# Attention and SoLU feed-forward on one core: loads of a whole batch in twelve transfers, block transposes one round sooner, weight conversion on VectorE

## The chip, the core and the metric

The kernel runs on one core of a Trainium2 chip. A core has a matrix engine (TensorE, "PE" in the profile, with its weight loads listed as "PEld"), a vector engine (VectorE, "DVE"), an engine for activation functions (ScalarE, "ACT"), a general engine (GpSimd, "POOL") and one that here only issues transfers (SyncE, "SP"). Each works through its own queue in program order and waits on semaphores for the others. Transfers between the chip's main memory and the on-chip memory, and within the on-chip memory, are issued from the queues of SP and ACT ("SPq" and "ACTq") and carried out by 16 DMA engines; an issue occupies the issuing engine's queue.

The metric is the device time of one execution in microseconds (us), as the median of several runs. A profile is of one execution.

## What is computed

Attention with a threshold, over 8 batches of 8 heads with 576 positions of 64 values, and then a feed-forward block over the 4608 rows of 512 values that come out of it. All of it is in 32-bit floating point; `w_in` and `w_out` arrive as 64-bit floating point.

```python
scores = scale * np.matmul(q, k.transpose(0, 1, 3, 2))
thresh = np.max(scores, axis=-1, keepdims=True) - tau
scores = np.where(scores >= thresh, scores, -1000000000.0)
scores = scores - np.max(scores, axis=-1, keepdims=True)
attn = np.exp(scores)
attn = attn / (np.sum(attn, axis=-1, keepdims=True) + 1e-09)
x = np.matmul(attn, v)          # then (B,H,S,D) -> (B*S, H*D)

h = x @ w_in
e = np.exp(h - np.max(h, axis=-1, keepdims=True))
sm = e / (np.sum(e, axis=-1, keepdims=True) + 1e-09)
solu = h * sm
ln = (solu - mean(solu)) / np.sqrt(var(solu) + 1e-06) * g_ln
out = ln @ w_out
```

## The kernel before

**Tiles and rounds.** Two heads form a pair, so a batch has four pairs. The 576 query positions are four tiles of 128 and a rest of 64; position 4p+t lies on partition p of tile t. A batch is worked in two halves. In half 0 each pair is a *unit* of two rounds (query tiles 0 and 1 of both heads), in half 1 a unit of three (tiles 2 and 3, then the two rests in one tile). That makes 20 rounds to a batch and 160 rounds in all, called slots, numbered from 0; batch b starts at slot 20 b. The whole order of work is written out by hand in one loop over rounds (from L541); nothing reorders it.

**One slot's way through the engines.** PE makes the scores of two tiles into two of three score banks (`scores`, L277). DVE takes the row maxima (`maxes`, L287), POOL adds tau (`nth`, L291), ACT shifts the scores out of the bank with a steep slope below the threshold (L304), which frees the bank, and exponentiates them with a row sum (L311). One round later POOL adds the small constant to the sum, DVE takes the reciprocal (L321), and POOL scales the probabilities (`normalise`, L323). Two rounds after the scores, DVE transposes 32 x 32 blocks of them into a tile T (`blocks`, L337). When a unit is complete, SP issues 16 transfers that put the blocks of T in place, into a tile wT (L345). Five rounds after the unit's last scores (`LAG_PV`, L485) PE multiplies wT with v (`attend`, L363), and ACT and DVE copy the result (L373 to L381).

**Loads and turns.** `load(i)` brings one pair: q and k in two transfers each, v in one, and a transfer each for the rests qe, ke and ve, eight in all (L108, L115, L119). For batch 0 the first two pairs go through SP's queue at the start; everything after goes through ACT's, at the top of a round, ahead of that round's `exps`, four rounds before the pair is turned. `prep(i, step)` turns a pair on PE in three steps (q, k, the rests; L223, L234) with copies to qT and kT on ACT (L229, L231) and of the rests to q_end and kT on DVE (L238, L242). The q and k tiles are double, the v tiles sevenfold.

**The feed-forward block** works on 36 tiles of 128 rows, each over four rounds: two halves of `ff_h` (PE, L399), `ff_max` (DVE, L406), `ff_exp` (ACT, L412), `ff_mul` (DVE, L418), `ff_stats` (DVE and POOL, L428 to L439), `ff_t`, which turns u on PE (L450) and copies it to uT on ACT or DVE (L453), two halves of `ff_o` (PE, L463), and `ff_out` (ACT, L470) with its store (L479).

**One round** issues, in this order: loads that are due, `scores` and `maxes` of this slot, one job of a list (attend before turning u before prep, by `x_next`), early jobs (`ff_max`), `exps` of this slot, `normalise` of the slot before, late jobs (`ff_exp`, `ff_mul`, `ff_stats`, `ff_out`), a quarter of the feed-forward matmuls, `blocks` of the slot two before, a second job of the list, and in the first rounds a weight piece.

**Weights.** 16 pieces of 128 x 512 are loaded as 64-bit words and converted by integer arithmetic: `weight_a` takes the exponent and the mantissa apart (L170 and L180 on DVE, L174 and L177 on POOL), `weight_b` puts the 32-bit number together (L194 to L200, DVE). One piece is converted per round, up to slot 14; `center` then subtracts the mean from w_out (L210, L212).

**Banks.** Jobs of the list (turned q and k, turned u, the attend result) share two banks, of which the feed-forward result holds one for two rounds. A bank is free when the copy that reads it has ended.

Of the kernel before, what the change touches and what calls it, by code (L numbers as in the profile page):

```python
# [16 lines left out]
P = 128  # L17
# [3 lines left out]
def kernel(  # L21
# [59 lines left out]

    pairs = {}
    units = {}
    xh = {}
# [15 lines left out]
    def load(i, queue=nc.scalar):  # L100
        b, hp = divmod(i, NP)
        d = {}
        for nm, src in (("q", q), ("k", k), ("v", v)):
            hs = src[b, 2 * hp : 2 * hp + 2]
            bufs = 7 if nm == "v" else 2
            if nm == "v":
                t = loads.tile([P, 2, 4, D], F32, tag=nm, bufs=bufs, name=nm)
                queue.dma_start(  # L108
                    out=t.rearrange("p h t d -> p h (t d)"),
                    in_=hs[:, 0:SM, :].rearrange("h (p t) d -> p h (t d)", t=4),  # L110
                )
            else:
                t = loads.tile([P, 4, 2, D], F32, tag=nm, bufs=bufs, name=nm)
                for h in range(2):
                    queue.dma_start(  # L115
                        out=t[:, :, h], in_=hs[h, 0:SM, :].rearrange("(p t) d -> p t d", t=4)
                    )
            e = loads.tile([ST, 2, D], F32, tag=nm + "e", bufs=bufs, name=nm + "e")
            queue.dma_start(out=e, in_=hs[:, SM:S, :].rearrange("h p d -> p h d"))  # L119
            d[nm], d[nm + "e"] = t, e  # L120
        pairs[i] = d
# [36 lines left out]
    def weight_load(x):  # L158
        raw = work.tile([P, 512], I64 if wide else F32, tag="u", name="raw")
        nc.scalar.dma_start(out=raw, in_=piece(x)[0])  # L160
        raws[x] = dict(raw=raw)

    def weight_a(x):
        if not wide:
            return
        d = raws[x]
        hi = d["raw"].bitcast(I32).rearrange("p (n two) -> p n two", two=2)[:, :, 1]
        d["em"] = em = work.tile([P, 2, 512], I32, tag="uT", name="em")
        e, m = em[:, 0], em[:, 1]
        nc.vector.tensor_scalar(  # L170
            out=e, in0=hi, scalar1=20, scalar2=0x7FF,
            op0=ALU.logical_shift_right, op1=ALU.bitwise_and,
        )
        nc.gpsimd.tensor_scalar(  # L174
            out=e, in0=e, scalar1=896.0, scalar2=0.0, op0=ALU.subtract, op1=ALU.max
        )
        nc.gpsimd.tensor_scalar(  # L177
            out=e, in0=e, scalar1=255.0, scalar2=8388608.0, op0=ALU.min, op1=ALU.mult
        )
        nc.vector.tensor_scalar(  # L180
            out=m, in0=hi, scalar1=0xFFFFF, scalar2=0x100000,
            op0=ALU.bitwise_and, op1=ALU.bitwise_or,
        )
# [32 lines left out]
    def prep(i, step):  # L216
        d = pairs[i]
        tag, tp = take_bank("tp_" + "qke"[step])
        banks_free.append(tag)
        if step < 2:  # L220
            nm = "qk"[step]
            for t in range(4):
                nc.tensor.transpose(  # L223
                    out=tp[:, P * t : P * t + P], in_=d[nm][:, t],
                    identity=ident,
                )
            d[nm + "T"] = heads.tile([P, SM if step == 0 else S], F32, tag=nm + "T", name=nm + "T")
            if step == 0:
                nc.scalar.activation(out=d["qT"], in_=tp, func=AF.Copy, scale=scl)  # L229
            else:  # L230
                nc.scalar.copy(out=d["kT"][:, 0:SM], in_=tp)  # L231
            return
        for x, nm in enumerate("qk"):
            nc.tensor.transpose(  # L234
                out=tp[:, ST * x : ST * x + ST], in_=d[nm + "e"], identity=ident[0:ST, 0:ST]
# [6 lines left out]
        nc.vector.tensor_copy(out=d["kT"][:, SM:S], in_=tp[:, ST : 2 * ST])  # L242

# [54 lines left out]
    def exps(s):  # L298
# [3 lines left out]
        for x, (ps, _) in enumerate(d["ps"]):  # L302
            w = work.tile([P, S], F32, tag="w", bufs=7, name="w")
# [46 lines left out]
    def attend(key):  # L350
        b, half, hp = key
        i = b * NP + hp
        d = pairs[i]
# [4 lines left out]
        for c in range(5):  # L358
            kk = slice(0, P if c < 4 else ST)
            for h in range(2):  # L360
                vv = d["v"][:, h, c] if c < 4 else d["ve"][:, h]
# [5 lines left out]
        if hp == 0:  # L367
            xh[b, half] = work.tile([P, NP, 256], F32, tag="xh", bufs=4, name="xh")
# [39 lines left out]
    def ff_exp(t):  # L408
        d = ffn[t]
        d["u"] = work.tile([P, DFF], F32, tag="u", name="u")  # L410
# [31 lines left out]
    def ff_t(t, f):  # L442
        d = ffn[t]
        if f == 0:
            d["uT"] = work.tile([P, NC, P], F32, tag="uT", name="uT")
# [42 lines left out]
    loads_due = []  # L488
    prepped = {}

    def prep_job(i, step):
        prep(i, step)
        prepped[i] = step

    for i in range(NPAIR):
        b, hp = divmod(i, NP)
        if b == 0:
            at = [max(0, 2 * hp - 3 + x) for x in range(3)]
            loads_due.append((0, i))
        else:  # L500
            s0 = PER_BATCH * (b - 1) + HALF0 + 3 * hp + 1
            at = [s0, s0 + 1, s0 + 2]
            loads_due.append((s0 - 4, i))
        if i > 0:
            for step in range(3):
                x_jobs.append([at[step], 2, (lambda i=i, step=step: prep_job(i, step))])
# [11 lines left out]
    with tc.manual_schedule():  # L518
        load(0, nc.sync)
        loads_due.pop(0)  # L520
# [3 lines left out]
        load(1, nc.sync)  # L524
        loads_due.pop(0)
        weight_a(0)
        for step in range(3):
            prep_job(0, step)
# [4 lines left out]
        done_w = 1  # L533

# [6 lines left out]
        while True:  # L541
            if rnd < NS:
                while (
                    loads_due
                    and loads_due[0][0] <= rnd
                    and prepped.get(loads_due[0][1] - 2) == 2
                ):
                    load(loads_due.pop(0)[1])
# [49 lines left out]
            if rnd - 2 >= 0 and rnd - 2 in live:  # L598
                blocks(rnd - 2)
# [44 lines left out]
```

## Time and profile before

| | |
|---|---|
| median of 3 runs | 1339.88 us (1337.8 to 1340.06) |
| the profiled execution | 1342.53 us |
| its span, first to last instruction | 1340.7 us |
| mean granted clock of PE | 0.888 of full |
| busy share of PE, DVE, ACT, POOL | 84%, 50%, 43%, 31% |
| moved by DMA | 132.05 MB, 98 GB/s on average |
| transfers wT from T | 1024, issued by SP |
| loads of q, k, v and their rests on ACT's queue | 240 |

A row of the timeline gives the start and the duration in us, the engine, the line, the operation, the tile written and the tiles read, and how many such instructions were merged; in brackets stands the time for which the engine was idle before it and what ended that. A row of the waits gives who waited for whom, the total in us, how often, and the longest. "issue" names a wait for which the profile shows no releaser. A busy PE may run below its full clock, so its share says how long it was occupied and not how much it did.

### The profile page before, as it was taken

How to read it: one execution, taken by the hardware profiler on the slowest of the kernel's cores; microseconds unless marked ns; L12 is line 12 of the kernel's file. 1: busy time of each engine (PE TensorE's matmuls, PEld its weight loads, DVE VectorE, ACT ScalarE, POOL GpSimd, SP SyncE). 2: the span in 40 equal slices, each digit the busy share in tenths (PEclk: the TensorE clock that was granted, in tenths of full speed). 3: DMA queues.
4: the chain of work that ended last, by engine and by line, in shares of the span. 5: the costliest groups of instructions: out<-in, count | busy, mean ns of one | idle time of the engine just before them, and what ended most of it. 6: DMA issues, size and time to landing. Idle time of an engine off the chain costs nothing.

```text
span 1340.7 us, 13897 instructions
## 1 busy us (share of the span) xinstructions
PE 1129.8 (84%) x4209; PEld 542.9 (40%) x4209; DVE 671.0 (50%) x1241; ACT 574.3 (43%) x1169; POOL 417.4 (31%) x833
## 2 busy tenths in 40 slices
PE   5566798888988889879888889889878889997878
PEld 3233343444434444434434434444434444443333
DVE  4665564535535556445544546454545546654312
ACT  2333244444535445444534445445444445543211
POOL 6667232322323223222222223232223223332100
PEclk8567898779889899879988999889998999998899
DMA  6556135334344443534363433544353433333210
GB/s 169 134 152 154 41 88 122 98 92 101 92 110 103 100 92 82 125 96 99 74 148 93 105 78 85 133 100 98 77 142 96 103 82 86 99 88 74 67 38 23
DMA packets 261738, 132.05 MB, mean 98 GB/s; under 512 B 99352, under 2 KB 255008, under 8 KB 261664
## 3 DMA queue, kind: packets, MB, share of 16 engines
q1 hardware_dynamic: 169632, 86.78, 28.0%
q10 hardware_dynamic: 92032, 44.39, 12.5%
q8 instruction: 34, 0.56, 0.2%
q14 instruction: 40, 0.33, 0.1%
HBM read 36.70 MB, written 9.44 MB: 34 GB/s over the span
## 4 chain that ended last, share of the span: by engine, by line
PE 51%; SPq 13%; ACT 9%; DVE 9%; DMA 8%; issue 5%; POOL 3%; ACTq 1%; DVEq 0%
PE pv L363 14%; PE h_ps L399 13%; SPq L345 12%; PE o_ps L463 11%; PE s_ps L277 9%; DMA wT<-T 5%; ACT w L304 3%; ACT w L311 3%; DVE T L337 3%; DVE u L418 2%; DVE nm L287 2%; PE tp_u L450 1%; ACT u L412 1%; POOL em L174 1%; DMA q<-in_q_dram 1%
## 5 line engine op out<-in xcount | busy, mean ns | idle before, releaser
L287 DVE TENSOR_REDUCE nm<-s_ps 128x1 f32<-128x576 f32 x288 | 204.4, 744 | 211.4 <-PE s_ps L277 211.2
L304 ACT ACTIVATE w<-s_ps,nth 128x576 f32<-128x576 f32 x288 | 199.3, 738 | 229.9 <-POOL nth L291 192.1
L277 PE MATMUL s_ps<-kT,qT 64*128 64x64 f32 (+1 forms) x1024 | 226.5, 485 | 81.2 <-ACT w L304 75.5
L463 PE MATMUL o_ps<-w,uT 128*128 128x512 f32 x576 | 274.5, 622 | 1.0 <-ACT uT L453 1.0
L323 POOL TENSOR_SCALAR w<-w,sm 128x576 f32<-128x576 f32 x288 | 214.0, 754 | 179.7 <-DVE sm L321 179.7
L363 PE MATMUL pv<-wT,v 128*64 128x384 f32 (+1 forms) x1024 | 198.5, 544 | 75.9 <-DMA wT<-T 44.7
L399 PE MATMUL h_ps<-w,xh 128*128 128x512 f32 x512 | 249.5, 633 | 0.0
L291 POOL TENSOR_SCALAR nth<-nm,tau_t 128x2 f32<-128x2 f32 (+1 forms) x160 | 47.9, 299 | 592.5 <-DVE nm L287 591.1
L311 ACT ACTIVATE w<-w,ntau 128x576 f32<-128x576 f32 x288 | 220.4, 772 | 1.0
L277 PEld LDWEIGHTS s_ps<-kT,qT 64*128 64x128 f32 x1024 | 126.2, 204 | 218.7 <-issue 96.1
L337 DVE STREAM_TRANSPOSE T<-w 128x576 f32<-128x576 f32 x288 | 207.0, 753 | 13.6 <-DMA wT<-T 8.0
L463 PEld LDWEIGHTS o_ps<-w,uT 128*128 128x128 f32 x576 | 108.7, 198 | 129.1 <-issue 125.4
L363 PEld LDWEIGHTS pv<-wT,v 128*64 128x64 f32 x1024 | 90.5, 170 | 148.4 <-issue 127.7
L399 PEld LDWEIGHTS h_ps<-w,xh 128*128 128x128 f32 x512 | 98.6, 203 | 116.5 <-issue 115.7
L378 ACT COPY xh<-pv 64x256 f32<-64x256 f32 x32 | 11.7, 365 | 187.1 <-PE pv L363 167.1
L418 DVE TENSOR_TENSOR u<-h_ps,u 128x1024 f32<-128x1024 f32 x36 | 44.1, 1224 | 91.0 <-ACT u L412 91.0
L373 ACT COPY xh<-pv 128x256 f32<-128x256 f32 x32 | 11.9, 372 | 157.6 <-PE pv L363 129.2
L380 DVE COPY xe<-pv 64x64 f32<-64x64 f32 x32 | 6.9, 215 | 140.5 <-ACT xh L379 140.4
L321 DVE RECIPROCAL sm<-sm 128x2 f32<-128x2 f32 (+1 forms) x160 | 26.1, 163 | 98.4 <-POOL sm L320 96.7
L450 PE MATMUL tp_u<-ident,u 128*128 128x128 f32 x288 | 48.5, 295 | 24.7 <-ACT uT L453 10.7
L311 ACT ACTIVATION_READ_ACCUMULATOR w<-w,ntau 128x1 f32 x288 | 56.5, 196 | 0.0
L450 PEld LDWEIGHTS tp_u<-ident,u 128*128 128x128 f32 x288 | 35.3, 150 | 48.8 <-issue 19.8
(62 smaller groups left out, 801.1 us busy)
## 6 DMA issues: line engine op xcount, KB each, us to landing
wT<-T SPq DMA_DIRECT2D x512, 80.0 KB, 2.2
wT<-T SPq DMA_DIRECT2D x256, 100.0 KB, 2.3
wT<-T SPq DMA_DIRECT2D x256, 64.0 KB, 2.1
out_dram<-ob ACTq DMA_DIRECT2D x32, 256.0 KB, 2.6
q<-in_q_dram ACTq DMA_DIRECT2D x60, 128.0 KB, 2.9
k<-in_k_dram ACTq DMA_DIRECT2D x60, 128.0 KB, 2.9
v<-in_v_dram ACTq DMA_DIRECT2D x30, 256.0 KB, 3.2
raw<-in_moe_w_in_dram ACTq DMA_DIRECT2D x8, 512.0 KB, 3.7
```

The lines of the kernel that those rows point to most:

```text
L277: nc.tensor.matmul(out=ps[:, ks], lhsT=lhsT, rhs=kT[hh, ks], start=True, stop=True)
L287: nc.vector.tensor_reduce(out=nm[:, x : x + 1], in_=ps[:, 0:S], axis=AX.X, op=ALU.max, negate=True)
L304: nc.scalar.activation(out=w, in_=ps[:, 0:S], func=AF.Prelu, bias=d["nth"][:, x : x + 1], scale=1.0, alpha=1.0e30,)
L311: nc.scalar.activation(out=w, in_=w, func=AF.Exp, bias=ntau, scale=1.0, accum_out=sm[:, x : x + 1])
L323: nc.gpsimd.tensor_scalar(out=w, in0=w, scalar1=d["sm"][:, x : x + 1], scalar2=1.0, op0=ALU.mult, op1=ALU.mult,)
L337: nc.vector.transpose(out=T[:, :, place, :], in_=w)
L345: nc.sync.dma_start(out=wT[32 * c : 32 * c + 32, 0:nj, a, :], in_=T[32 * a : 32 * a + 32, c : NB : 4].rearrange("p j t q -> p j (t q)"),)
L363: nc.tensor.matmul(out=y[hh, 0 : 4 * nq], lhsT=vv, rhs=wT[kk, c, :, 64 * h : 64 * h + nq], start=c == 0, stop=c == 4,)
L399: nc.tensor.matmul(out=h[:, f], lhsT=x[:, c], rhs=w1[:, c, f], start=c == 0, stop=c == NP - 1)
L418: nc.vector.tensor_tensor(out=d["u"], in0=d["h"], in1=d["u"], op=ALU.mult)
L450: nc.tensor.transpose(out=tp[:, P * c : P * c + P], in_=d["u"][:, x : x + P], identity=ident)
L463: nc.tensor.matmul(out=d["o"], lhsT=d["uT"][:, c], rhs=w2[:, c], start=c == 0, stop=c == NC - 1)
```

## The change

There are three parts and some tiles that make room for them.

1. **Loads.** `load(b)` brings a whole batch in twelve transfers: q and k in four each (one per tile t, all heads), and one each for v, qe, ke and ve. It is a generator that is advanced once per round, so that a round issues at most two of them, over seven rounds; it starts when all pairs of the batch before are turned. For batch 0, q and k come in one transfer per head, q on SP's queue and k on ACT's. The q and k tiles of a batch are single, those of v double.
2. **Order.** `blocks` takes the slot one before instead of two before, in the round in which that slot is normalised. `LAG_PV` is unchanged. The w tiles go from seven to five.
3. **Weight conversion.** The two operations on POOL go to DVE.

Raw weights use the tiles xh2 and xh3, the exponents and mantissas u and uT; u and uT are single where they were double.

```diff
-    def load(i, queue=nc.scalar):
-        b, hp = divmod(i, NP)
+    def load(b):
         d = {}
         for nm, src in (("q", q), ("k", k), ("v", v)):
-            hs = src[b, 2 * hp : 2 * hp + 2]
-            bufs = 7 if nm == "v" else 2
+            bufs = 2 if nm == "v" else 1
+            e = loads.tile([ST, H, D], F32, tag=nm + "e", bufs=bufs, name=nm + "e")
...
+        if b == 0:
+            for h in range(H):
+                for nm, src, queue in (("q", q, nc.sync), ("k", k, nc.scalar)):
+                    queue.dma_start(
+                        out=d[nm][:, :, h], in_=src[b, h, 0:SM, :].rearrange("(p t) d -> p t d", t=4)
+                    )
+                if h == 1:
...
+                    yield
+        else:
+            for nm, src in (("q", q), ("k", k)):
+                for t in range(4):
+                    nc.scalar.dma_start(
+                        out=d[nm][:, t],
+                        in_=src[b, :, 0:SM, :].rearrange("h (p t) d -> t p h d", t=4)[t],
+                    )
+                    if t % 2:
+                        yield
+                nc.scalar.dma_start(
+                    out=d[nm + "e"], in_=src[b, :, SM:S, :].rearrange("h p d -> p h d")
                 )
+                yield
+        nc.scalar.dma_start(
+            out=d["v"].rearrange("p h t d -> p h (t d)"),
+            in_=v[b, :, 0:SM, :].rearrange("h (p t) d -> p h (t d)", t=4),
+        )
+        nc.scalar.dma_start(out=d["ve"], in_=v[b, :, SM:S, :].rearrange("h p d -> p h d"))
+        yield
...
-        nc.gpsimd.tensor_scalar(
+        nc.vector.tensor_scalar(
             out=e, in0=e, scalar1=896.0, scalar2=0.0, op0=ALU.subtract, op1=ALU.max
         )
-        nc.gpsimd.tensor_scalar(
+        nc.vector.tensor_scalar(
             out=e, in0=e, scalar1=255.0, scalar2=8388608.0, op0=ALU.min, op1=ALU.mult
         )
...
-            w = work.tile([P, S], F32, tag="w", bufs=7, name="w")
+            w = work.tile([P, S], F32, tag="w", bufs=5, name="w")
...
-        d["u"] = work.tile([P, DFF], F32, tag="u", name="u")
+        d["u"] = work.tile([P, DFF], F32, tag="u", bufs=1, name="u")
...
-            d["uT"] = work.tile([P, NC, P], F32, tag="uT", name="uT")
+            d["uT"] = work.tile([P, NC, P], F32, tag="uT", bufs=1, name="uT")
...
-        load(0, nc.sync)
-        loads_due.pop(0)
+        first = load(0)
+        next(first)
         constants()
         weight_load(0)
         weight_load(1)
-        load(1, nc.sync)
-        loads_due.pop(0)
+        for _ in first:
+            pass
         weight_a(0)
...
-                while (
-                    loads_due
-                    and loads_due[0][0] <= rnd
-                    and prepped.get(loads_due[0][1] - 2) == 2
-                ):
-                    load(loads_due.pop(0)[1])
+                if loaded + 1 < B and rnd >= PER_BATCH * loaded and turned == NP * (loaded + 1):
+                    loaded += 1
+                    loading = load(loaded)
+                next(iter(loading), None)
                 scores(rnd)
                 maxes(rnd)
...
-            if rnd - 2 >= 0 and rnd - 2 in live:
-                blocks(rnd - 2)
+            if rnd >= 1 and rnd - 1 in live:
+                blocks(rnd - 1)
```

61 lines of the change are left out of this document (29 added, 32 removed).

## The prediction

> **What bounds the kernel now.** I read the page's first parts, then a table of stages, then who waits for whom, then the timeline at the waits.
>
> ```profile
> PE 1129.8 (84%) x4209; PEld 542.9 (40%) x4209; DVE 671.0 (50%) x1241; ACT 574.3 (43%) x1169; POOL 417.4 (31%) x833
> ...
> PE 51%; SPq 13%; ACT 9%; DVE 9%; DMA 8%; issue 5%; POOL 3%; ACTq 1%; DVEq 0%
> ```
>
> TensorE (PE) is the fullest engine, but only half of the chain that ended last is PE. The table of stages (columns: stretch, its length, busy time of PE, PEld, DVE, ACT, POOL, granted clock, DMA share, GB/s) shows two regimes, the weight stage, then one batch like another:
>
> ```profile
> 0.00:128.70 128.70, 77.53 (x252) 41.87 (x252) 77.32 (x150) 45.62 (x92) 84.63 (x90) 0.67 0.58 151
> 345.80:499.20 153.40, 132.10 (x505) 63.32 (x504) 75.80 (x141) 70.61 (x144) 42.88 (x96) 0.90 0.42 100
> 1109.40:1250.30 140.90, 127.55 (x496) 59.08 (x496) 74.80 (x135) 65.45 (x135) 42.43 (x97) 0.94 0.33 80
> ```
>
> In the first 128.7 us POOL is the fullest; later PE is, with about 21 us of waiting per batch (153.4 less 132.1) at a clock below 1. The waits of PE after 160 us:
>
> ```profile
> PE pv L363 <- DMA wT<-T: 42.7, 15, 4.8
> PE s_ps L277 <- ACT w L304: 40.2, 21, 6.0
> PE pv L363 <- issue: 30.9, 8, 5.4
> PE tp_u L450 <- ACT uT L453: 10.7, 3, 5.5
> ```
>
> So two things stop PE: probabilities that arrive late (wT), and an ACT that is late with the shift of the scores (L304), whose end frees the score banks.
>
> **Block transposes a round sooner.** One late wT, slot 53 of the 160 rounds (POOL, DVE, SP's queue, PE):
>
> ```profile
> 458.03 0.74 POOL L323 TENSOR_SCALAR w<-w,sm 128x576 f32<-128x576 f32 x1 [0.29 <-DVE sm L321]
> ...
> 471.17 0.77 DVE L337 STREAM_TRANSPOSE T<-w 128x576 f32<-128x576 f32 x1
> ...
> 472.00 10.59 SPq L345 DMA_DIRECT2D wT<-T  x16
> ...
> 484.70 4.38 PE L363 MATMUL pv<-wT,v 128*64 128x384 f32 x16 [3.06 <-DMA wT<-T]
> ```
>
> The input was scaled at 458.8, yet its transpose ran at 471.2, because it stood behind the next round's feed-forward work on DVE. Then SP needs 10.6 us to issue 16 transfers, and PE lost 3.06 us. A round sooner it could run at about 459.5, which moves the landing forward by some 11 us, more than the longest wait (4.8). SP can take it: it holds nothing but wT transfers after the start, and it idles long enough for T:
>
> ```profile
> SPq L345 <- DVE T L337: 503.2, 49, 31.2
> ```
>
> The wT buffer of two units before is freed by an attend that stands earlier in the same round, so I cost that at nothing; uncovered it would be one pv block, 3 to 4 us of SP. Gain: 42.7 us, and of the eight "issue" waits two that are also wT. The other six are 3.82 us each (22.9 of 30.9) and stay: PE there wants a bank that DVE's last copy frees:
>
> ```profile
> 438.80 0.23 DVE L242 COPY kT<-tp_e 128x64 f32<-128x64 f32 x1
> ...
> 439.13 2.73 PE L363 MATMUL pv<-wT,v 128*64 128x256 f32 x16 [3.82 <-issue]
> ...
> 442.84 5.73 PE L463 MATMUL o_ps<-w,uT 128*128 128x512 f32 x8
> ```
>
> So 42.7 + 8.0 = **50.7 us**, in 17 waits.
>
> **Loads.** Today a pair's eight transfers stand in a row on ACT's queue, ahead of that round's exps:
>
> ```profile
> 229.47 1.30 ACTq L115 DMA_DIRECT2D k<-in_k_dram  x2
> 231.96 0.63 ACTq L119 DMA_DIRECT2D ke<-in_k_dram  x1
> ...
> 233.95 1.37 ACT L304 ACTIVATE w<-s_ps,nth 128x576 f32<-128x576 f32 x2 [6.93 <-DMA k<-in_k_dram]
> ...
> 234.75 1.85 PE L277 MATMUL s_ps<-kT,qT 64*128 64x512 f32 x3 [3.82 <-ACT w L304]
> ...
> 542.41 0.90 PE L450 MATMUL tp_u<-ident,u 128*128 128x128 f32 x3 [5.53 <-ACT uT L453]
> ...
> 1001.08 1.85 PE L277 MATMUL s_ps<-kT,qT 64*128 64x512 f32 x2 [6.01 <-ACT w L304]
> ```
>
> Each issue is about 0.63 us of ACT's sequencer, with a pause (230.77 to 231.96) where an issue waited. Afterwards a batch has 12 issues in place of 32, at most two (1.3 us) in a round. The PE waits of this kind: four on L304, first 3.82 and last 6.01, 19.8 us together, and two on uT (10.0 of the 10.7 us). **29.8 us**, in 6 waits. The remaining issues: today's 36 output tiles are stored by single short issues, after which PE has the waits of the second row:
>
> ```profile
> 453.51 0.36 ACTq L479 DMA_DIRECT2D out_dram<-ob  x1
> ...
> PE tp_u L450 <- ACT ob L470: 3.0, 4, 1.0
> ...
> q<-in_q_dram ACTq DMA_DIRECT2D x60, 128.0 KB, 2.9
> ```
>
> That is 0.083 us of PE per 0.36 us of issue; 49 groups (seven rounds in each of seven batches) of up to 1.3 us cost by that row about 49 x 0.083 x 3.6 = **15 us** back (nothing, if ACT's idle time covers all; 64 us if every group reaches PE). The q and k tiles are now single, but the next load waits until all four pairs are transposed, which is some eight rounds ahead of its first reader; the last k transfer still has some three. A transfer is 256 KB rather than 128 KB: today's land in 2.9 us (third row), and three rounds of 7.7 us (153.4 / 20) hide even four times that.
>
> **Clock.** A wait costs PE more than itself. After the 3.82 us above, eight o_ps matmuls took 5.73 us; undisturbed:
>
> ```profile
> 430.31 3.60 PE L463 MATMUL o_ps<-w,uT 128*128 128x512 f32 x8
> ...
> 460.94 2.80 PE L363 MATMUL pv<-wT,v 128*64 128x384 f32 x16
> ```
>
> That is 2.1 us more, and after the 3.06 us wait sixteen pv took 4.38 in place of 2.80, 1.6 more. I take 1.85 us for 21 of the 23 waits removed (the two shortest, under 2 us, left out): **38.9 us**. The Trainium skill (page TensorE: Matmul & The Clock Gate, section HAM oscillation — how this bites in real kernels) lets the clock fall only behind idle gaps longer than about 3.4 us; by that rule ten waits count (the four longest on wT, up to the 4.8 and 5.4 in the rows above, and the six of the loads) and the term is 18.5 us, not 38.9. The row of 3.06 us speaks against so sharp a limit, so I keep 21.
>
> **DVE's new wait.** Now each transpose follows POOL's scaling in the same round. The weight stage shows the order:
>
> ```profile
> 44.46 0.17 DVE L321 RECIPROCAL sm<-sm 128x2 f32<-128x2 f32 x1 [2.46 <-POOL sm L320]
> 44.54 1.42 DVE L337 STREAM_TRANSPOSE T<-w 128x576 f32<-128x576 f32 x2
> 45.89 0.84 DVE L194 SCALAR_TENSOR_TENSOR w<-raw,em 128x512 f32<-128x512 uint32 x1
> ...
> 47.98 0.42 DVE L170 TENSOR_SCALAR em<-raw 128x512 int32<-128x512 int32 x1
> 48.31 0.42 DVE L180 TENSOR_SCALAR em<-raw 128x512 int32<-128x512 int32 x1
> 48.65 1.41 DVE L287 TENSOR_REDUCE nm<-s_ps 128x1 f32<-128x576 f32 x2
> 53.26 0.17 DVE L321 RECIPROCAL sm<-sm 128x2 f32<-128x2 f32 x1 [3.20 <-POOL sm L320]
> ...
> 44.73 1.47 POOL L323 TENSOR_SCALAR w<-w,sm 128x576 f32<-128x576 f32 x2 [0.30 <-DVE sm L321]
> 48.48 2.03 POOL L174 TENSOR_SCALAR em<-em 128x512 int32<-128x512 int32 x1 [2.29 <-DVE em L170]
> 50.60 1.93 POOL L177 TENSOR_SCALAR em<-em 128x512 int32<-128x512 int32 x1
> 52.63 0.30 POOL L291 TENSOR_SCALAR nth<-nm,tau_t 128x2 f32<-128x2 f32 x1
> ...
> DVE nm L287 <- PE s_ps L277: 211.2, 80, 9.8
> ```
>
> The columns are start, duration, engine, line; the fence has DVE's rows, then POOL's, then one row of DVE's waits. Transposes that end at 45.96 would end at 44.73 + 1.47 + 0.77 = 46.97 (POOL's two scalings, then the second transpose): 1.0 us later. Queued behind them on DVE are the copies of q_end, kT and uT, which free banks, and the next round's max, on which nth, L304 and PE's next scores hang. In 72 rounds (36 tiles, two each) feed-forward work on DVE fills the gap; 88 remain. In half of all rounds (80 of 160) DVE is 2.6 us ahead of PE and hides it. So 44 x 1.0 = **44 us** back; between nothing and 88.
>
> **Weight stage.** The round is 8.80 us (reciprocal at 44.46, the next at 53.26), because nth stands on POOL behind two conversions of 2 us. On DVE they are the same kind of operation on the same tile as L170 and L180, which follow each other every 0.34 us; I take that. The new round, from reciprocal to reciprocal: transposes end after 2.51, three conversions 2.09 (45.89 to 47.98), four more 4 x 0.34 = 1.36, max 1.41, then 0.1 + 0.63 (52.63 to 53.26) for nth and the sum, and every third round some 0.8 us of copies: 8.4 us. DVE takes POOL's place as the bound: 0.4 x 13 rounds = 5 us gained. At 0.77 us an operation, the spacing after L194, the round is 10.1, and 13 x 1.3 = 17 us are lost. At the start ACT issues eleven more transfers before its first copy (11 x 0.63 = 7 us), but the block of eight that round 0 has today (5 us) goes: -2, with 5 us either way. Batch 1 is then loaded in rounds 6 to 12, its k and ke right ahead of their transposes, where two landings of 2.9 us may show: -3, from -6 to 0. Together **0** (from -30 to +8).
>
> **Single buffers.** u and uT go from two buffers to one, w from seven to five. The exp that rewrites u stands two rounds behind the transposes that read it, PE's own order puts the last reader of uT ahead of the transposes of the next tile, and w is free a round sooner. I cost that at nothing; if a cover failed, a wait like the 5.53 us on uT above would return.
>
> **Sum.** 50.7 + 29.8 + 38.9 + 0 - 15 - 44 = 60.4 us. The profiled execution took 1342.53 us (its span is 1340.7); the median of three, 1339.88, is 2.65 us below it. 1342.53 - 60.4 - 2.65 = 1279.5, so **1279 us**.
>
> **Rivals.**
> - Only wT gains: the loads still hold ACT, as an issue beside a wT burst waits in turn (the pause at 230.77). 50.7 + 15 x 1.85 - 15 - 44 = 19 us: 1320. For it: SP's 10.6 us of issue nearly fill a unit of two rounds; against: never more than two in a row. 0.16.
> - DVE's slack hides its wait: no 44 us, 1235. For it: DVE is 50% busy; against: it also waits for ACT and POOL. 0.14.
> - Only long gaps slow the clock: ten of the 21 waits exceed 3.4 us, so 11 x 1.85 = 20 us less, 1299. 0.06. The rule of the Trainium skill's page named above gives this.
> - **Slower**: DVE's wait for the scaling becomes the bound. Where max comes late PE waits for L304, and from some 2.5 us of waiting the clock falls too: 1.0 + 1.85 = 2.85 us a round. All else gains 104 us, so it decides from 37 rounds; at 50 of the 88 it is 142 us, a loss of 38: 1378. For it: in the weight stage DVE is already the next bound; against: the 2.6 us lead. 0.15.
> - The same rival near its turning point: no change beyond 0.2%, which is about what a measurement of this kernel can tell apart. 0.05.
>
> **How the numbers follow.** Forecast 0.44, its own range 1245 to 1310. Faster 0.44 + 0.16 + 0.14 + 0.06 = 0.80, same 0.05, slower 0.15. The range of 1215 to 1350 starts where nothing is given back and the weight stage gains its 8 us (1279 - 59 - 8 = 1212), takes in the weight stage at its worst (1309) and the second case, and ends just inside the slower case; it leaves out most of that case and a little below, about 0.2.
>
> **What would show it.** PE's waits on wT nearly gone, and pv's landing margin near 10 us: the first step. No ACT wait on a load over 2 us: the second. Batches of about 144 us in place of 153 and a clock near 0.93: the third. DVE's T waiting for POOL L323 about 1 us a time: the fourth. Rounds of 8.4 us in the first 130 us: the fifth. It is wrong if PE's waits on L304 grow past 80 us, or if T's waits are several us long.

## The result and the profile after

| | before | changed |
|---|---|---|
| median of 4 runs, us | 1339.97 (1337.8 to 1341.46) | 1224.29 (1221.78 to 1225.07) |
| profiled execution, us | 1342.53 | 1225.07 |
| its span, us, and mean granted clock | 1340.7, 0.888 | 1223.2, 0.935 |

The ratio is 0.9135, with a 95% interval of 0.9116 to 0.9153: 115.7 us are gained where 60 were forecast. The time lies inside the range, near its lower end. Line numbers of the changed kernel are 24 to 29 above those of before (L304 becomes L333, L337 becomes L366).

The page's first parts of the changed kernel, busy times and chain:

```profile
PE 1090.5 (89%) x4209; PEld 525.1 (43%) x4209; DVE 690.2 (56%) x1273; ACT 574.8 (47%) x1169; POOL 350.8 (29%) x801
...
PE 53%; DVE 13%; DMA 9%; ACT 8%; SPq 6%; issue 5%; POOL 4%; ACTq 1%; DVEq 0%
```

PE's share of the span has gone from 84 to 89%, and SP's queue has lost more than half of its share of the chain (13 to 6%). The table of stages says more. I cut each run where PE starts the first scores of batch 1 (slot 20). Before that the weights are converted; behind it every batch does the same work. First the two rows of before, then those of the changed kernel (length, then busy times of PE, PEld, DVE, ACT and POOL):

```profile
0.00:192.30 192.30, 128.27 (x408) 65.34 (x408) 109.96 (x213) 67.82 (x137) 105.48 (x124) 0.72 0.50 125
192.30:1340.70 1148.40, 1001.57 (x3803) 477.55 (x3802) 561.08 (x1029) 506.52 (x1032) 311.89 (x709) 0.92 0.39 94
```

```profile
0.00:182.93 182.93, 125.00 (x408) 64.04 (x408) 124.20 (x247) 68.33 (x137) 39.61 (x92) 0.88 0.58 135
182.93:1223.20 1040.27, 965.46 (x3803) 461.08 (x3802) 566.01 (x1027) 506.44 (x1032) 311.17 (x709) 0.94 0.46 103
```

The first stage is 9.4 us shorter, the rest 108.1. The same 3803 matmuls take 965.5 us in place of 1001.6. These 36.1 us are clock: added up from the trace's records of the granted clock, PE was busy at half clock for 172.6 us of this stretch before and for 100.9 after, and half of the difference is 35.8. The other 72.0 us are PE's idle time (length less busy: 146.8, then 74.8). Which waits went, by PE's waits after 160 us, is to be read against the rows shown for before:

```profile
PE pv L391 <- issue: 18.9, 6, 3.2
PE s_ps L306 <- ACT w L333: 14.5, 12, 2.7
PE pv L391 <- ACT ob L498: 10.7, 13, 1.4
...
PE pv L391 <- DMA wT<-T: 6.6, 6, 2.2
...
PE tp_u L478 <- ACT uT L481: 0.7, 1, 0.7
```

On wT PE waits 6.6 us in place of 42.7, on L333 14.5 in place of 40.2, on uT 0.7 in place of 10.7. A new wait of 10.7 us has come behind the old one: pv now waits for the bank that ob's copy frees. DVE's waits show the price of the edit, first the changed kernel's:

```profile
DVE nm L316 <- PE s_ps L306: 104.3, 60, 6.2
...
DVE T L366 <- POOL w L352: 71.6, 82, 0.9
```

The transposes do wait for POOL's scaling, 82 times and 0.87 us each (71.6 / 82). They lie in 82 rounds, none of which has the feed-forward multiplication or statistics in the gap. DVE's wait for PE's scores, 211.2 us before, has fallen to 104.3. Part of that is only the shorter run; how much of the new wait was put where DVE had waited anyway is measured below, with the scaling done twice and left out.

### The profile page after: what moved, and what is told of

It is laid out like the page before. It is cut to its first block, busy times and chain, and to the rows that moved or that the text cites. A ratio compares the mean times of both kernels' runs of the same rounds, so it can differ in the third digit from the quotient of the medians.

```text
span 1223.2 us, 13714 instructions
## 1 busy us (share of the span) xinstructions
PE 1090.5 (89%) x4209; PEld 525.1 (43%) x4209; DVE 690.2 (56%) x1273; ACT 574.8 (47%) x1169; POOL 350.8 (29%) x801
## 4 chain that ended last, share of the span: by engine, by line
PE 53%; DVE 13%; DMA 9%; ACT 8%; SPq 6%; issue 5%; POOL 4%; ACTq 1%; DVEq 0%
PE o_ps L491 14%; PE h_ps L427 13%; PE pv L391 13%; PE s_ps L306 9%; SPq L374 6%; DMA wT<-T 5%; DVE T L366 5%; DVE nm L316 4%; ACT w L333 3%; POOL w L352 2%; ACT w L340 2%; DMA q<-in_q_dram 2%; PE tp_u L478 1%; ACT ob L498 1%; POOL nth L320 1%
## 5 line engine op out<-in xcount | busy, mean ns | idle before, releaser
L333 ACT ACTIVATE w<-s_ps,nth 128x576 f32<-128x576 f32 x288 | 199.3, 738 | 203.1 <-POOL nth L320 188.0
L316 DVE TENSOR_REDUCE nm<-s_ps 128x1 f32<-128x576 f32 x288 | 204.1, 743 | 104.7 <-PE s_ps L306 104.3
L366 DVE STREAM_TRANSPOSE T<-w 128x576 f32<-128x576 f32 x288 | 212.6, 767 | 86.5 <-POOL w L352 71.6
L306 PE MATMUL s_ps<-kT,qT 64*128 64x64 f32 (+1 forms) x1024 | 224.0, 483 | 35.9 <-ACT w L333 28.8
L352 POOL TENSOR_SCALAR w<-w,sm 128x576 f32<-128x576 f32 x288 | 211.4, 745 | 145.9 <-DVE sm L350 145.9
L427 PE MATMUL h_ps<-w,xh 128*128 128x512 f32 x512 | 243.5, 620 | 0.2 <-ACT w L333 0.2
L391 PE MATMUL pv<-wT,v 128*64 128x384 f32 (+1 forms) x1024 | 173.4, 488 | 36.2 <-issue 18.9
L427 PEld LDWEIGHTS h_ps<-w,xh 128*128 128x128 f32 x512 | 96.1, 198 | 112.2 <-issue 111.2
L391 PEld LDWEIGHTS pv<-wT,v 128*64 128x64 f32 x1024 | 78.7, 153 | 98.8 <-issue 70.3
L446 DVE TENSOR_TENSOR u<-h_ps,u 128x1024 f32<-128x1024 f32 x36 | 44.1, 1224 | 91.0 <-ACT u L440 91.0
L401 ACT COPY xh<-pv 128x256 f32<-128x256 f32 x32 | 11.9, 372 | 131.6 <-PE pv L391 128.6
L391 PE MATMUL pv<-wT,ve 64*64 64x256 f32 (+1 forms) x256 | 52.6, 491 | 0.0
```

Of the source, the lines that this page charges most:

```text
L306: nc.tensor.matmul(out=ps[:, ks], lhsT=lhsT, rhs=kT[hh, ks], start=True, stop=True)
L316: nc.vector.tensor_reduce(out=nm[:, x : x + 1], in_=ps[:, 0:S], axis=AX.X, op=ALU.max, negate=True)
L333: nc.scalar.activation(out=w, in_=ps[:, 0:S], func=AF.Prelu, bias=d["nth"][:, x : x + 1], scale=1.0, alpha=1.0e30,)
L352: nc.gpsimd.tensor_scalar(out=w, in0=w, scalar1=d["sm"][:, x : x + 1], scalar2=1.0, op0=ALU.mult, op1=ALU.mult,)
L366: nc.vector.transpose(out=T[:, :, place, :], in_=w)
L391: nc.tensor.matmul(out=y[hh, 0 : 4 * nq], lhsT=vv, rhs=wT[kk, c, :, 64 * h : 64 * h + nq], start=c == 0, stop=c == 4,)
```

## Experiments

Each kernel was timed beside the kernel before, both on the same chip; that one's median was 1337.4 to 1340.4 us throughout.

### Each part by itself

Four kernels lie between the two: the transposes alone added to before; the changed kernel with them undone; with the conversion undone; with both undone (loads by batch alone). The kernels with the conversion and without the loads by batch were not run.

The transposes alone, in the kernel before:

```diff
-            if rnd - 2 >= 0 and rnd - 2 in live:
-                blocks(rnd - 2)
+            if rnd >= 1 and rnd - 1 in live:
+                blocks(rnd - 1)
```

> The kernel before with one edit: the block transposes one round sooner; loads and weight conversion as before. Theory A (the prediction's working): the 17 waits on wT go with their clock, 50.7 + 31 us, and the transposes' wait for the scaling gives back 44: about 38 us, so 1302 us. Theory B (DVE's slack hides that wait): nothing is given back, 82 us, 1258 us. In both PE's waits on wT fall from 42.7 us to a few, and the waits of s_ps on ACT's L304 stay near 40 us, as the loads are untouched.

The changed kernel with the transposes undone:

```diff
-            w = work.tile([P, S], F32, tag="w", bufs=5, name="w")
+            w = work.tile([P, S], F32, tag="w", bufs=7, name="w")
...
-            if rnd >= 1 and rnd - 1 in live:
-                blocks(rnd - 1)
+            if rnd - 2 >= 0 and rnd - 2 in live:
+                blocks(rnd - 2)
```

> The changed kernel with the transposes two rounds late again (seven w buffers, as before): what is left are the loads and the conversion. Theory A: 38 us above the changed kernel's 1224, so 1262. Theory B: 82 us above, 1306. If neither, and the loads gain far more than the 41 us before their give-back, it stays below 1250.

With the conversion undone (in weight_a, both operations on e):

```diff
-        nc.vector.tensor_scalar(
+        nc.gpsimd.tensor_scalar(
             out=e, in0=e, scalar1=896.0, scalar2=0.0, op0=ALU.subtract, op1=ALU.max
         )
-        nc.vector.tensor_scalar(
+        nc.gpsimd.tensor_scalar(
             out=e, in0=e, scalar1=255.0, scalar2=8388608.0, op0=ALU.min, op1=ALU.mult
         )
```

> The changed kernel with the two conversion operations back on POOL. The prediction's working: 5 us for the rounds, so about 1229. The changed kernel's rounds of 8.1 us against 8.8 would say 0.7 x 13 = 9 us, 1233. If the conversion only moved the bound, 1224. The stall in round 10 on batch 1's k should stay in any case.

With both of the last two edits:

> The changed kernel with both other edits undone: only the loads by batch (and the single buffers). Theory A: 29.8 + 11 us less 15 for the issues that stay and 5 for the start and batch 1's k: about 20 us, 1320. Theory B (issues of at most 1.3 us are hidden by ACT's idle time): 35 to 41 us, about 1302. If the loads cost in the weight stage what they gain later, 1335 or more.

Measured: 1278.64 us (ratio 0.9497 to 0.9583), 1306.9 (0.9715 to 0.9801), 1245.84 (0.926 to 0.934) and 1327.21 (0.9842 to 0.993). Their rows of the table of stages, cut at slot 20 as above, in the same order:

```profile
0.00:202.08 202.08, 128.47 (x408) 65.71 (x408) 110.74 (x215) 67.61 (x137) 102.94 (x124) 0.71 0.50 122
202.08:1273.70 1071.62, 977.22 (x3803) 467.62 (x3802) 567.01 (x1027) 506.63 (x1032) 311.90 (x709) 0.94 0.42 100
```

```profile
0.00:180.38 180.38, 129.61 (x407) 66.95 (x407) 123.43 (x245) 68.14 (x137) 42.12 (x92) 0.84 0.58 134
180.38:1305.60 1125.22, 982.43 (x3803) 467.46 (x3802) 561.32 (x1029) 506.28 (x1032) 311.19 (x709) 0.93 0.42 96
```

```profile
0.00:206.97 206.97, 133.10 (x407) 67.25 (x408) 110.54 (x215) 68.55 (x137) 102.92 (x124) 0.84 0.51 119
206.97:1244.20 1037.23, 963.11 (x3803) 458.91 (x3802) 565.81 (x1027) 506.47 (x1032) 311.92 (x709) 0.95 0.46 103
```

```profile
0.00:200.41 200.41, 134.23 (x408) 69.12 (x408) 109.93 (x213) 68.56 (x137) 105.46 (x124) 0.83 0.51 120
200.41:1329.00 1128.59, 991.59 (x3803) 470.14 (x3802) 561.24 (x1029) 506.21 (x1032) 311.89 (x709) 0.92 0.42 96
```

Put together (the rest is the stage behind slot 20; idle is its length less PE's busy time):

| blocks | loads | conversion | median, us | first stage | rest | PE idle in the rest |
|---|---|---|---|---|---|---|
| | | | 1339.97 | 192.3 | 1148.4 | 146.8 |
| x | | | 1278.64 | 202.1 | 1071.6 | 94.4 |
| | x | | 1327.21 | 200.4 | 1128.6 | 137.0 |
| | x | x | 1306.90 | 180.4 | 1125.2 | 142.8 |
| x | x | | 1245.84 | 207.0 | 1037.2 | 74.1 |
| x | x | x | 1224.29 | 182.9 | 1040.3 | 74.8 |

Three things follow by subtraction of rows.

- **The transposes** gain 61 us on the kernel before and 82 on the one with loads by batch. Behind slot 20 that is 77 to 91 us; in the first stage they cost 2.5 to 10 us. Theory A's 38 us is refuted. Theory B's 82 is met where they are undone (1306.9 against 1306); added to the kernel before they bring 21 us less than that (1278.64 against 1258), 9.8 of them in the first stage. There PE's wait on wT fell to 1.3 us, as expected. The wait on L304 did not stay near 40 but fell to 32.8, and the one on uT from 10.7 to 1.8, although the loads were untouched.
- **The conversion** gains 20 to 22 us, 20 to 24 in the first stage and nothing behind it. I had expected none, 5 or 9.
- **The loads** gain 20 us behind slot 20 without the transposes and 34 with them, and lose 5 to 8 in the first stage. By themselves they give 1327.21 us, between theory A (1320) and the 1335 of a weight stage that takes back what the loads gain; theory B (1302) is refuted. The seven runs spread from 1313 to 1332. Without the transposes part of the gain only became more waiting for wT. PE's waits of the kernel with loads alone, after 160 us, beside 42.7 and 40.2 us before:

```profile
PE pv L391 <- DMA wT<-T: 58.5, 21, 5.2
...
PE s_ps L306 <- ACT w L333: 15.3, 13, 2.7
```

How the conversion gains 20 us stands in its timeline. POOL of the changed kernel with the conversion undone, one round from one conversion to the next, then DVE of the changed kernel:

```profile
57.62 2.03 POOL L198 TENSOR_SCALAR em<-em 128x512 int32<-128x512 int32 x1 [3.14 <-DVE em L194]
59.74 1.93 POOL L201 TENSOR_SCALAR em<-em 128x512 int32<-128x512 int32 x1
61.77 0.30 POOL L320 TENSOR_SCALAR nth<-nm,tau_t 128x2 f32<-128x2 f32 x1
...
62.66 1.47 POOL L352 TENSOR_SCALAR w<-w,sm 128x576 f32<-128x576 f32 x2 [0.30 <-DVE sm L350]
67.27 2.03 POOL L198 TENSOR_SCALAR em<-em 128x512 int32<-128x512 int32 x1 [3.14 <-DVE em L194]
```

```profile
42.79 0.42 DVE L194 TENSOR_SCALAR em<-raw 128x512 int32<-128x512 int32 x1
43.24 0.43 DVE L198 TENSOR_SCALAR em<-em 128x512 int32<-128x512 int32 x1
...
44.38 1.41 DVE L316 TENSOR_REDUCE nm<-s_ps 128x1 f32<-128x576 f32 x2
...
52.50 1.41 DVE L316 TENSOR_REDUCE nm<-s_ps 128x1 f32<-128x576 f32 x2
```

With the transposes a round sooner, POOL and DVE stand in one ring: scaling, transposes, words of the weights, conversion on POOL, nth, sum, reciprocal, scaling. The ring takes 9.65 us (57.62 to 67.27), not the 8.80 of before: the transposes' wait for the scaling is in it. With the conversion on DVE (0.43 us an operation in place of 2.03) a round is 8.12 us (44.38 to 52.50). So 1.5 us a round, over 13 rounds 20 us. The same 1.5 us are gained without the transposes: from max to max on DVE the median round (slots 1 to 12) is 8.82 us with the loads alone and 7.28 with loads and conversion. So in the weight stage the two edits add up: the conversion takes 1.5 us off a round, the transposes put 0.8 on. The prediction's 8.4 us was the round with both, and its 5 us was what the one gains less what the other costs.

### What a microsecond of DVE's new wait costs

The scaling was done twice, and then left out:

```diff
         for x, w in enumerate(d["w"]):
+            nc.gpsimd.tensor_scalar(
+                out=w, in0=w, scalar1=1.0, scalar2=1.0, op0=ALU.mult,
+                op1=ALU.mult,
+            )
             nc.gpsimd.tensor_scalar(
                 out=w, in0=w, scalar1=d["sm"][:, x : x + 1], scalar2=1.0, op0=ALU.mult,
```

> The changed kernel; POOL scales each w tile twice (first by 1.0), so every transpose on DVE waits some 1.5 us longer in its round; results unchanged. Theory A (a wait of DVE reaches PE in half the rounds, 44 of 88 without feed-forward work): 1.5 x 80 = 120 us in all rounds, or 44 x 1.5 + 20 for the weight stage = 86: 1310 to 1344. Theory B (DVE's slack hides it after the weight stage, and only the 13 weight rounds, which are DVE's own chain, grow): 13 x 1.5 = 20 us, 1244; the time from slot 20 to the end stays at 1040 us.

> The changed kernel without POOL's scaling of w by the reciprocal of the sums (the probabilities stay unnormalised), so no transpose waits for POOL. Theory A: the 44 us given back and 13 in the weight stage come off: about 1167. Theory B: only the weight stage gains, 13 x 1.0 = 13 us: about 1211; from slot 20 on 1040 us as now.

Measured: 1262.79 us (1256.68 to 1275.42; 0.9382 to 0.9502) and 1194.99 (0.8882 to 0.8963). Neither theory is met: the first lies nearer to B (1244) than to A (1310), the second between A (1167) and B (1211), nearer to B. DVE's waits after 190 us, first with no scaling, then changed, then scaled twice:

```profile
DVE nm L316 <- PE s_ps L306: 148.1, 77, 7.0
```

```profile
DVE nm L316 <- PE s_ps L306: 102.7, 57, 6.2
...
DVE T L366 <- POOL w L352: 59.4, 68, 0.9
```

```profile
DVE T L370 <- POOL w L356: 145.9, 141, 1.4
...
DVE nm L316 <- PE s_ps L306: 39.4, 19, 5.1
```

The first stage of the kernel with two scalings ends at 203.5 us; behind it T's wait is 142.8 us. About three quarters of each step of T's wait come out of the wait for PE: 59.4 us more of the one are 45.4 less of the other, then 83.4 more are 63.3 less. Their rows behind slot 20, without the scaling and with it twice:

```profile
171.72:1191.70 1019.98, 954.21 (x3803) 454.27 (x3802) 555.75 (x1027) 506.76 (x1032) 126.19 (x456) 0.96 0.46 105
```

```profile
203.45:1273.60 1070.15, 978.06 (x3803) 468.55 (x3802) 565.68 (x1027) 507.88 (x1032) 482.03 (x963) 0.94 0.44 100
```

Three points: with 0, 59.4 and 142.8 us of that wait, the rest takes 1020.0, 1040.3 and 1070.2 us. That is about a third of a microsecond per microsecond (20.3 / 59.4 and 29.9 / 83.4); 9.0 and 17.3 us of it are PE's idle time, the remainder its clock. The second slope is an upper one: the profiled run was the slowest of its four (1275.42 against a median of 1262.79), and the second scaling also held up another operation on DVE, the feed-forward reciprocal, whose wait for POOL grew from 11.5 to 45.3 us. By the medians, less the first stage, both steps are 18 us (0.30 and 0.22 per microsecond).

Of the 17.3 us of idle time 15.3 are PE's waits for ACT's shift of the scores (14.5 us, then 29.8). So what reaches PE takes the path that was forecast: late transposes, a late max, a late shift. POOL did not hold nth up by itself; it started 0.10 us behind the max in both kernels.

In the first stage, where DVE sits in the ring above, there is no slack: with 0, 12.2 and 28.3 us of T's wait it is 171.7, 182.9 and 203.5 us long.

### What the remaining load issues cost

```diff
-                    nc.scalar.dma_start(
-                        out=d[nm][:, t],
-                        in_=src[b, :, 0:SM, :].rearrange("h (p t) d -> t p h d", t=4)[t],
-                    )
+                    for hs in (slice(0, H // 2), slice(H // 2, H)):
+                        nc.scalar.dma_start(
+                            out=d[nm][:, t, hs],
+                            in_=src[b, hs, 0:SM, :].rearrange("h (p t) d -> t p h d", t=4)[t],
+                        )
```

> The changed kernel with each q and k transfer of batches 1 to 7 in two halves (four heads each): 20 issues per batch in place of 12, up to four (2.5 us) in a round. The prediction's price of the issues that stay (0.23 us of PE per us of issue on ACT, 15 us in all): about 56 issues more x 0.6 x 0.23 = 8 us and, with four in a row, up to 15: 1232 to 1239. If ACT's idle time covers them (nothing given back): 1224, and PE's waits of s_ps on ACT L333 stay at 14.5 us after 160 us.

Measured: 1226.35 us (1216.9 to 1229.41; ratio 0.9089 to 0.9198), so 2 us above the changed kernel's median, within what the runs scatter. PE's waits on L334 (L333 there) after 160 us rose from 14.5 to 21.3 us, and its idle time behind slot 20 by 4 us (74.8 to 78.9). The rest did not get longer (1037.8 us), because its matmuls took 6.5 us less; the clock made up for the waits. The upper end of the interval is 1233 us (0.9198 x 1340.4): 15 us are excluded, 8 us lie at its edge. So the lower price of 8 us is neither shown nor refuted.

### Where to put the bank copies

The issue waits of 3.15 us that were left end with a copy on DVE. DVE of the changed kernel at one of them (PE waits until the kT copy's end at 262.6):

```profile
259.98 1.23 DVE L446 TENSOR_TENSOR u<-h_ps,u 128x1024 f32<-128x1024 f32 x1 [3.22 <-ACT u L440]
261.12 0.77 DVE L366 STREAM_TRANSPOSE T<-w 128x576 f32<-128x576 f32 x1
261.81 0.54 DVE L265 TENSOR_SCALAR q_end<-tp_e,scl 64x64 f32<-64x64 f32 x2
262.37 0.23 DVE L269 COPY kT<-tp_e 128x64 f32<-128x64 f32 x1
```

```diff
-            if rnd >= 1 and rnd - 1 in live:
-                blocks(rnd - 1)
             x_next(1 if rnd >= 4 else 2, rnd)
+            if rnd >= 1 and rnd - 1 in live:
+                blocks(rnd - 1)
```

> The changed kernel with the second turn of PE's side jobs (transposes of q, k and u with their copies) ahead of the block transposes in each round, so the bank copies on DVE no longer stand behind a transpose that waits for POOL. If the six issue waits of 3.15 us come from the transposes ahead of the kT copies, they go with their clock: 18.9 + 6 x 1.85 = 30 us, 1194. If the copies then wait for PE and hold the transposes (wT lands later), PE's waits on wT come back, and the time stays at 1224 or rises.

Measured: 1210.72 us (0.9007 to 0.9081). PE's waits after 160 us, and the rest behind slot 20:

```profile
PE pv L391 <- issue: 15.1, 7, 2.5
...
PE pv L391 <- DMA wT<-T: 5.0, 5, 1.4
```

```profile
183.95:1207.40 1023.45, 955.24 (x3803) 460.40 (x3802) 561.51 (x1027) 506.32 (x1034) 311.41 (x710) 0.96 0.46 105
```

The waits did not go: they are 2.50 us, shorter by the one transpose. The multiplication of u (L446) ahead of them still holds the copies. wT did not come later. The rest is 16.8 us shorter, 10.2 of them clock. By the medians 13.6 us are gained, less than half of the 30 that were expected if the waits went.

### The first stage

Batch 1's loads were taken three steps a round; the diff replaces `next(iter(loading), None)` by three calls while `loaded == 1`.

> The changed kernel with batch 1's loads in three steps of the generator per round in place of one (k issued by round 8 in place of 10). If the waits of tp_k and tp_e on k and ke in rounds 10 and 11 (12.7 + 2.2 us) only come from the late issue, they go: 15 us and up to 5 us of clock, 1205 to 1210, and slot 20 starts at about 166 us in place of 183. If DVE's chain of 8.1 us rounds takes their place as the bound, half or less: 1216 or more.

Measured: 1225.98 us (0.9128 to 0.9185), no gain. The waits on k were gone, but PE's waits on L333 in the first stage rose from 16.1 to 31.0 us, because ACT's queue could not issue sooner without holding what stands behind it:

```profile
78.98 5.59 ACTq L130 DMA_DIRECT2D k<-in_k_dram  x4
...
86.65 1.37 ACT L333 ACTIVATE w<-s_ps,nth 128x576 f32<-128x576 f32 x2 [9.97 <-DMA k<-in_k_dram]
```

The four issues took 5.59 us, as the later ones waited for earlier transfers to land, and the shift of the scores stood 9.97 us behind it: the very wait that the change took out of the later batches.

Next, batch 0's k of heads 2 to 7, v and ve went to SP's queue:

```diff
-                for nm, src, queue in (("q", q, nc.sync), ("k", k, nc.scalar)):
+                for nm, src, queue in (("q", q, nc.sync), ("k", k, nc.scalar if h < 2 else nc.sync)):
...
-        nc.scalar.dma_start(
+        tail = nc.sync if b == 0 else nc.scalar
+        tail.dma_start(
             out=d["v"].rearrange("p h t d -> p h (t d)"),
...
-        nc.scalar.dma_start(out=d["ve"], in_=v[b, :, SM:S, :].rearrange("h p d -> p h d"))
+        tail.dma_start(out=d["ve"], in_=v[b, :, SM:S, :].rearrange("h p d -> p h d"))
```

> The changed kernel with the k transfers of heads 2 to 7 and v and ve of batch 0 on SP's queue instead of ACT's, so that ACT's first copy of qT does not stand behind eight issues. If those issues are what puts the first scores at 18.4 us in place of 12.9, they start at about 13 and the time falls by 5 us, 1219. If the chain of DVE's rounds (8.1 us each) or pair 1's later k absorbs it, 1224.

Measured: 1217.36 us (0.9044 to 0.9127), 6.9 below the changed kernel. The first scores of the changed kernel, then of this one:

```profile
18.39 3.39 PE L306 MATMUL s_ps<-kT,qT 64*128 64x512 f32 x8
```

```profile
13.59 2.80 PE L307 MATMUL s_ps<-kT,qT 64*128 64x512 f32 x6 [0.27 <-ACT kT L259]
```

So the issues ahead of ACT's first copy were the late start. Of the 6.9 us, 3.1 lie in the first stage (182.9 us, then 179.9).

Then three things together: copies first, the start on SP, and batch 1's loads on SP too, two steps a round (every `dma_start` of load(b) on nc.sync for b < 2, but for k of heads 0 and 1 and ke of batch 0).

> The changed kernel with three things together: copies ahead of the block transposes; batch 0's later loads on SP's queue; batch 1's loads on SP's queue too, two steps of the generator per round. If batch 1's stall (14.9 us) came from ACT's queue, which can issue neither sooner without holding the exps, and SP can: 1211 - 5 - 15 = 1191. If the stall only moves again, into SP's wT transfers: 1206 or more.

Measured: 1203.21 us (1196.99 to 1211.35; 0.891 to 0.9024). The first two would add up to 1204 by themselves, so batch 1 on SP gained nothing that can be seen. The stall on k shrank from 12.7 to 5.0 us and came back on SP: in round 12 a pv waited 4.8 us for wT.

Last, batch 1's transposes came due two rounds later, in place of sooner loads:

```diff
-            s0 = PER_BATCH * (b - 1) + HALF0 + 3 * hp + 1
+            s0 = PER_BATCH * (b - 1) + HALF0 + 3 * hp + (3 if b == 1 else 1)
```

> The changed kernel with copies ahead of the block transposes and batch 0's later loads on SP's queue, as in the run of three together, but batch 1's loads as in the changed kernel; in their place batch 1's transposes of q, k and their ends come due two rounds later (from round 11 in place of 9), which their first reader in round 20 allows. The first two edits alone would add up to 1224.3 - 13.6 - 6.9 = 1204. If PE then no longer meets batch 1's k before it landed, and nothing takes the wait's place, the 12.7 + 2.2 us go: 1189. If DVE's rounds of 8.1 us hold the weight stage up to round 14 in any case, 15 rounds x 8.1 us less the 6 rounds before would leave less than half: 1197 to 1204.

Measured: **1195.16 us** (median of 6, 1193.58 to 1202.88; ratio 0.891 to 0.8985), between the two expectations, and the fastest here beside the one without the scaling. Its rows:

```profile
0.00:175.76 175.76, 128.45 (x399) 65.76 (x400) 122.96 (x243) 67.72 (x136) 39.66 (x92) 0.85 0.61 141
175.76:1193.30 1017.54, 948.71 (x3812) 458.12 (x3811) 561.98 (x1030) 506.88 (x1033) 311.90 (x709) 0.97 0.46 105
```

By the medians 9 us are gained on the sum of 1204, which was not run itself. The 14.9 us of waiting for k and ke are gone; in their place PE waits longer for L334 in rounds 11 and 12 (24.7 us in the first stage, against 15.7 with only the start on SP). Slot 20 starts 4.1 us sooner than with only the start on SP (175.8 against 179.9), so about half of the 9 us lies there. The other half is PE's pace behind slot 20, and what caused it is not shown.

## Why the prediction came out as it did

The direction, the parts that gain and their order were right; the gain is nearly twice the forecast. By its steps:

- **Transposes, 50.7 us**: right. Waits on wT fell by 36.1 us and issue waits by 12.0, 48.1 together; with the transposes alone it was 41.4 and 11.9. The six issue waits that were to stay at 3.82 stayed, at 3.15. A landing margin near 10 us was too much: from the last wT landing to the first pv the median over the 56 units behind batch 0 went from 2.1 to 6.7 us (worked out from the landing of each unit's sixteen transfers). What came next, pv's wait for ob's copy (10.7 us), I had not named.
- **Loads, 29.8 us**: right in the sum, 25.7 (L304) and 10.0 (uT), but these waits were not the loads' alone: with the transposes alone 7.4 and 8.9 us of them went too. ACT's waits for transfers of k and ke, 107.5 us in nine groups before, became one of 3.6 us.
- **Clock, 38.9 us**: right in size, 36.1 by PE's busy time behind slot 20, and 35.8 by the records of the clock.
- **Remaining issues, -15 us**: not borne out. The row that I priced them by (waits beside the output stores) was, as it says, a wait on ob's copy, not on an issue, so the price had no basis. Doubled, they came with 4 us more of PE's idle time and no difference in the median that shows; up to 8 us are not excluded.
- **DVE's new wait, -44 us**: this is the step that failed. Its size and count were right (82 waits of 0.87 us against 88 of 1.0), and so was the path by which it reaches PE; that half of it does was not. Behind slot 20 a microsecond of it cost between a fifth and a third of one. All that the scaling costs there is 20.3 us, and of that the wait is a part. The row of DVE's waits for PE (211.2 us) held the answer: I read its count (80 of 160 rounds) as the rounds that are covered, and the others as uncovered in full. That a wait is also covered by slack that comes later, on PE or before the next scores are needed, fits this but was not followed round by round.
- Together: 50.7 + 29.8 + 38.9 = 119.4 us of gross gain stand against 108.1 measured behind slot 20. By this account 11 us were given back, not 59, which is 48 of the 55 us by which the forecast was off. It is an estimate, as its gross gain is the forecast one; what the runs bound is the scaling's part, 20.3 us at most.
- **Weight stage, 0**: 9.4 us gained, with three terms off. The round was 8.1 us, not 8.4: by the starts of DVE's maxima the way from slot 0 to slot 14 took 8.4 us less, where 5 less 3 were forecast. The start was 5.5 us later (first scores at 18.39 in place of 12.87; the first max 5.8 later), not 2. Between slots 14 and 20 another 6.8 us were gained, for which I had no term. PE waited 14.9 us for batch 1's k and ke, but DVE sets the round there: the two rounds concerned took 8.47 and 8.82 us beside 8.13, so the 3 us forecast as lost are not contradicted.
- **Single buffers, 0**: PE's wait on uT is 0.7 us. No run undid them alone, so that is not shown separately.
- **Rivals**: the nearest was that DVE's slack hides its wait (1235). That only wT gains is refuted by the table (the loads gain 34 us with the transposes). The slower one, 2.85 us a round from 37 rounds on, is refuted by the doubled scaling: T's wait 2.4 times as long behind slot 20 still gave 1262.8 us.

## What to carry to other kernels

A new wait on an engine that also waits for others is to be charged against that other wait first: here 60 us of it cost some 20, and doubling and removing the awaited operation measured the slope in two runs. The same wait costs in full where the engine lies in a closed ring, as in the weight stage, so split the sum by stage. And when two edits lie on one ring, price each by itself: what was forecast as 5 us for both together was 20 us gained by the conversion and about 10 lost by the transposes.

## What the runs showed of the hardware

The clock does not fall behind a fixed length of wait. The kernel with the transposes alone has six issue waits of 3.16 us, at the same place of six batches. Behind two of them pv kept its full pace, behind four it did not. One of each, PE's timeline:

```profile
289.99 1.95 PE L363 MATMUL pv<-wT,v 128*64 128x256 f32 x16 [3.16 <-issue]
```

```profile
433.87 2.89 PE L363 MATMUL pv<-wT,v 128*64 128x256 f32 x16 [3.16 <-issue]
```

The same sixteen pv took 1.95 us and 2.89. In the changed kernel a wait of 2.65 us was enough; behind it the eight scores take 3.02 us, where undisturbed they take 1.30:

```profile
230.79 3.02 PE L306 MATMUL s_ps<-kT,qT 64*128 64x512 f32 x8 [2.65 <-ACT w L333]
```

By the records of the granted clock in the traces of both kernels and all experiments, behind 190 us, half clock followed within 3.4 us on 39 of 39 pv waits of 3.28 us or more, on 58 of 66 from 2.6 to 3.28 us, and on 32 of 47 from 1.8 to 2.6 (in 6 of these it had begun before the wait). So a shorter wait lowers the chance of a slow stretch, without a sharp limit below 3.28 us.

The records also show what a fall goes with. In each of the fourteen traces every change of the granted clock lies on a grid of 3.413 us, to within 0.002 us; the grid's offset differs from run to run. The two waits above lie differently on the grid. Two windows of it for the first wait, then two for the second (PE's busy time stands first, the granted clock third from the end):

```profile
287.94:291.36 3.42, 1.38 (x14) 1.15 (x16) 3.24 (x7) 0.00 (x0) 0.06 (x1) 1.00 0.75 178
291.36:294.77 3.41, 3.41 (x16) 1.45 (x13) 2.12 (x6) 2.21 (x5) 2.56 (x7) 1.00 0.50 123
```

```profile
431.30:434.72 3.42, 0.85 (x8) 0.74 (x10) 3.39 (x7) 0.00 (x0) 0.00 (x0) 1.00 0.65 144
434.72:438.13 3.41, 3.41 (x16) 1.58 (x12) 2.10 (x6) 0.27 (x2) 2.20 (x5) 0.50 0.57 140
```

The first wait is split between two windows, and PE is busy for 40% of the emptier one; the second leaves 25% of its window, and the clock is halved at the window's end. Over all fourteen traces, of the windows at full clock behind 190 us, all 154 in which PE was busy for under 40% were followed by half clock, 78 of 242 between 40 and 70%, and 19 of 3436 above. Of these 19, 18 were busy for some 88%, with scores and pv alone or nearly so; why the clock fell there is open.

The Trainium skill (TensorE: Matmul & The Clock Gate, section What's actually happening) has a free-running window of 3413 ns behind the gate. The grid of 3.413 us agrees with it, and so does that a wait of one length comes out both ways. A sharp limit of 3.4 us on the wait, the rival from the same page at 1299, does not agree with the row of 2.65 us.
